# A three-stage float32 kernel on one core: one quad instead of two by whole float32 matmuls, and elementwise work of the first blocks on GpSimd

## The chip, the cores and the metric

The kernel runs on one core of a Trainium2 chip. The metric is the device time of one execution in microseconds, as the median of several runs. The profile is taken from one further execution; its span runs from the first to the last instruction of the core, and that execution's device time is a little longer than its span.

## The reference, cut to what matters

A linear attention is followed by two feed-forward networks. All inputs and the output are float32. B = 4 batches, H = 8 heads, S = 576 rows, D = 64; so 2304 tokens of 512 values go through two networks with 2048 hidden values.

```
q_s = softmax(q, over the head's 64 values);  k_s = softmax(k, over the sequence)
kv  = k_s^T v                  # 64 x 64 for each batch and head
x   = q_s kv                   # heads side by side: 2304 x 512
h1  = x @ w_in1 ; g1 = softplus(h1) ; y = g1 @ w_out1
h2  = y @ w_in2 ; g2 = elu(h2)      ; out = g2 @ w_out2
```

## The kernel before

The 2304 tokens are cut into six blocks of 384 rows, and two blocks make a pair (three pairs). The hidden values of a network are cut into eight quarters of 256, called f = 0 to 7. A **quad** (m, p, f) is the work of network m, pair p and quarter f: an up product (512 to 256 values, over the pair's two blocks), an activation, and a down product that adds into PSUM. There are 2 x 3 x 8 = 48 quads, and they follow each other in the order m, p, f; the down product of one quad is laid between the up products of the next.

An ordinary quad works with seven products in place of eight (a Strassen-like scheme). It needs seven *forms* of x for the pair (`add_forms`: four differences `ts`, line 599, and for each form a high part, line 588, and a low part, line 592, as the products are made from a rounded high part and a low remainder), seven forms of the up weights (`add_w_in`: four sums `st`, line 711, high parts by ScalarE, line 727, low parts by VectorE, line 731), a high and a low part of the down weights (`add_w_out`, lines 751 and 755), and of the activation (`add_g`, lines 940 and 944). Its up products (line 811) leave seven results that ScalarE copies (line 824) and VectorE adds (line 845).

A **direct** quad leaves all that out: `add_up_direct` (line 872) and the `whole` branch of `add_down` (line 1011) multiply float32 tiles as they are, and its activation stands in `g` alone. Before, the quads (0, 0, 0) and (0, 0, 1) are direct:

```
direct = lambda m, p, f: (m, p) == (0, 0) and f < 2
```

For the eight quarters of each network the weights are first turned from the words of the input into float32 by `add_words` (ScalarE lines 647 and 661, VectorE lines 651, 655 and 672); they come through the ring `raw` of two buffers. In network 0 the up forms are made anew for each pair from the turned words, and the down parts are stored in DRAM and loaded again.

Before the first quad the attention of block 0 must be done (`add_k`, `add_q` for four pairs of heads, each by itself), then that of block 1 (two units of four heads). In `add_q` the row maximum (line 439) is subtracted (line 446), ScalarE takes the exponential (line 452), VectorE sums (456) and multiplies by the reciprocal (line 476, `qn`). Block 0's subtractions are on GpSimd already, the rest of this is on VectorE. The values then pass through TensorE (lines 491 and 507) into `sx`, the pair's x.

All instructions are put in order by a planner (`Plan.order`), which simulates the engines with a duration for each step (`t_act`, `t_dve`, `t_pool`, `t_dma`) and takes the step that can start first, and among those that can start together the most urgent. `PRI` is a table of numbers that make groups of steps more urgent (k00 is k of block 0's heads 0 and 1, k12 the second unit of block 1, x00 the forms of pair 0, i0 to i7 and o0 to o7 the weights of a quarter). All DMAs are issued by SyncE, in the planned order. GpSimd has, beside the subtractions, the `memset` of line 304, which waits until TensorE has read the buffer `v` (line 375).

Of the kernel before, what the change touches and what calls it, by code (L numbers as in the profile page):

```python
# [12 lines left out]
ALU = mybir.AluOpType  # L13
# [132 lines left out]


def t_pool(n):
    return 0.15 + n / 476


def t_dma(n):
# [4 lines left out]
def attention_moe_moe_kernel(  # L157
# [93 lines left out]

    SLOT = 15.7
    UP, DN = 6 * 0.175, 3 * 0.231
    direct = lambda m, p, f: (m, p) == (0, 0) and f < 2
    quads = [(m, p, f) for m in range(2) for p in range(NPAIR) for f in range(NQ)]
    start, now = {}, 45.0
    for m, p, f in quads:
# [4 lines left out]
    def after_quad(m, p, f):  # L262
        i = quads.index((m, p, f)) + 1
        return start[quads[i]] if i < len(quads) else end


    kload = {}
# [147 lines left out]
    def add_q(t, hps, behind=()):  # L415
# [23 lines left out]
            nc.vector.tensor_reduce(new(qm)[:, : 2 * R * G], flat(), axis=AX.X, op=ALU.max)  # L439

        N = 2 * R * G
        eng = POOL if early else DVE

        @step(eng, 1.1 if early else t_dve(n), r=[qm], w=[qk])
        def _(eng=eng):
            (nc.gpsimd if eng == POOL else nc.vector).tensor_tensor(
                flat(), flat(), T[qm][:, :N].to_broadcast([P, N, D]), op=ALU.subtract
            )

# [18 lines left out]
        by = lambda t: t[:, :n].rearrange("p (g h r d) -> p g h r d", g=G, h=2, r=R)  # L468
        rows = lambda: T[qk][:, BLK:] if early else T[nk][:, :n]

        @step(DVE, t_dve(n), r=[qk, qd], w=[nk] if early else [], make=[] if early else [(nk, "u")])
        def _():
            if not early:
                new(nk)
            for g in range(G):
                nc.vector.tensor_tensor(
                    rows()[:, g * BLK : (g + 1) * BLK].rearrange("p (r h d) -> p h r d", h=2, r=R),
                    by(T[qk])[:, g],
                    T[qd][:, 2 * R * g : 2 * R * (g + 1)].rearrange("p (h r) o -> p h r o", h=2).to_broadcast([P, 2, R, D]),
                    op=ALU.mult,  # L480
                )
# [85 lines left out]
    def add_forms(m, p):  # L567

        t = (2 * p, 2 * p + 1)

        def b(i, j):
            return [("xs", m, t[j - 1], kc) for kc in (2 * i - 2, 2 * i - 1)], ("sx", m, t[j - 1]), (
                lambda: T["sx", m, t[j - 1]][:, (i - 1) * 2 * BLK : i * 2 * BLK]
            )

        def ts(i):
            key = ("ts", m, p, i)
            return [key], key, (lambda: T[key])

        def form(i, src):  # L580
            r, hold, view = src
            xk, hk, lk = (("x" + c, m, p, i) for c in "fhl")
            part = lambda j: T[xk][:, j * 2 * BLK : (j + 1) * 2 * BLK]

            @step(ACT, t_act(2 * BLK), r=r, w=[hk], make=[(xk, "xf")], hold=[hold], line="xf")
            def _():
                new(xk)
                nc.scalar.copy(part(0), view())

            @step(DVE, t_dve(2 * BLK), r=[*r, hk], w=[lk], hold=[xk, hold])  # L590
            def _():
                nc.vector.tensor_tensor(part(1), view(), part(0).bitcast(F32), op=ALU.subtract)

        def diff(i, one, two):
            key = ("ts", m, p, i)

            @step(DVE, t_dve(2 * BLK), r=[*one[0], *two[0]], make=[(key, "ts")], hold=[one[1], two[1]], line="ts")
            def _():
                nc.vector.tensor_tensor(new(key), one[2](), two[2](), op=ALU.subtract)

            return ts(i)

        form(1, b(1, 1))
        form(2, b(2, 1))
        t1 = diff(1, b(1, 2), b(1, 1))
        t2 = diff(2, b(2, 2), t1)
        form(6, t2)
        form(5, t1)
        form(3, b(2, 2))
        t3 = diff(3, b(2, 2), b(1, 2))  # L610
        form(7, t3)
        t4 = diff(4, b(2, 1), t2)
        form(4, t4)
# [78 lines left out]
    def add_w_in(m, p, f, rk):  # L692
# [9 lines left out]
            (3, lambda: a(1, 1), lambda: a(2, 1), ALU.subtract), (4, lambda: a(1, 2), lambda: s(2), ALU.subtract),  # L702
        ]
        for i, x, y, op in sums:
            @step(
                DVE, t_dve(W2), r=[rk], w=[] if i == 1 else [sk], make=[(sk, "st")] if i == 1 else [],
            )
            def _(i=i, x=x, y=y, op=op):
                if i == 1:
                    new(sk)  # L710
                nc.vector.tensor_tensor(s(i), x(), y(), op=op)

        view = lambda j, lo, n, c: T[wk][:, j * 7 * W2 + lo : j * 7 * W2 + lo + n].rearrange(
            "p (c n) -> p c n", c=c
# [138 lines left out]
    def add_up_direct(f):  # L853
        t0 = start[0, 0, f]
        wk = ("w", "ti", 0, "i", f)
        for t in range(2):
            gk = ("g", 0, 0, f, t)
            for j in range(2):
                key = ("up", f, t, j)
                for lo in range(0, KC, PART):  # L860
                    kcs = range(lo, lo + PART)

                    @step(
                        PE, PART * 0.645, r=[wk, *(("xs", 0, t, kc) for kc in kcs)], w=[key] if lo else [],
                        make=[] if lo else [(key, "ha")], hold=[("sx", 0, t)],
                        due=t0 + (4 * t + 2 * j + lo / 2) * (UP + 1.5 * DN), line=("up", t) if lo + PART == KC else None,
                    )
                    def _(key=key, j=j, t=t, kcs=kcs):
                        ps = T[key] if kcs[0] else new(key)
                        for kc in kcs:  # L870
                            lo = kc * W2 + j * P
                            nc.tensor.matmul(  # L872
                                ps[:, :BLK], T[wk][:, lo : lo + P], sx(0, t, kc),
                                start=(kc == 0), stop=(kc == KC - 1),
                            )

                last_up[0, 0, f] = _

                @step(
                    ACT, t_act(BLK, True), r=[key], w=[gk] if j else [],  # L880
                    make=[] if j else [(gk, "gh" if f else "g")], line=("g", t), tab="sp",
                )
                def _(key=key, gk=gk, j=j):
                    if not j:
                        new(gk, F32)
                    softplus(T[gk][:, j * BLK : (j + 1) * BLK], T[key][:, :BLK])
# [96 lines left out]

    def add_down(m, p, f):

        wk = ("wo", m, "o", f) if p == direct(m, 0, f) else ("wo", m, "o", f, p)
        t0 = after_quad(m, p, f)
        if turned(m, p):
            return add_down_turned(m, p, f, wk, t0)
# [4 lines left out]
        for (i, j, r), at in zip(order, fill):  # L994
# [2 lines left out]
            hk, lk, ak = ("gh", m, p, f, i), ("gl", m, p, f, i), ("acc", m, p, half, r)  # L997
            first = f == 0 and j == 0

            whole = direct(m, p, f)  # L1000
            gk, w32 = ("g", m, p, f, i), ("w", "ti", m, "o", f)

            @step(
# [18 lines left out]
    def add_store(m, p):  # L1022
# [55 lines left out]


    PRI = dict(  # L1080
        k00=97, q00=38, k01=54, q01=13, k02=167, q02=154, k03=94, q03=54, k10=9, q10=83, k12=24, q12=11,
        k20=157, q20=11, k22=95, q22=30, k30=136, q30=45, k32=30, q32=0, x00=6, x01=36, x02=32, x10=48, x11=48,
        x12=213, y=59, w=-34, ahead=148, i0=-2, i1=43, i2=48, i3=173, i4=-23, i5=52, i6=66, i7=17, o0=105,
        o1=26, o2=29, o3=-28, o4=45, o5=18, o6=-2, o7=10,
    )

    def early(kind):
# [25 lines left out]
    for i, (m, p, f) in enumerate(quads):  # L1113
# [8 lines left out]
            load_w_in(m, p, f)  # L1122
        if (m, p) == (0, 0):
            early(f"o{f}")
        if direct(m, p, f):
            add_words(m, "o", f, "wo")
        elif (m, p) == (0, 0):
            add_w_out(m, f, add_words(m, "o", f))
        elif p == (1 if direct(m, 0, f) else 0):
            add_w_out(m, f, load_words(m, p, "o", f))  # L1130
        else:
            load_w_out(m, p, f)
# [4 lines left out]
        early(None)  # L1137
        if direct(m, p, f):
            add_up_direct(f)
        else:  # L1140
            add_up(m, p, f)
            for j in range(2):
# [47 lines left out]
```

## Time and profile before

| | |
|---|---|
| median of 3 runs | 842.51 us (842.42 to 843.38) |
| the profiled execution | 843.36 us, its span 841.3 us |
| TensorE busy | 821.2 us (98% of the span) |
| VectorE, ScalarE, GpSimd busy | 590.1, 534.2, 6.1 us |

Busy shares are means over the whole span. The two networks don't load the engines alike, and the first pair, whose attention, forms and words fall together, loads VectorE and ScalarE far more than the rest; so the first 200 us are to be read by stages.

### The profile page before, as it was taken

How to read it: one execution, taken by the hardware profiler on the slowest of the kernel's cores; microseconds unless marked ns; L12 is line 12 of the kernel's file. 1: busy time of each engine (PE TensorE's matmuls, PEld its weight loads, DVE VectorE, ACT ScalarE, POOL GpSimd, SP SyncE). 2: the span in 40 equal slices, each digit the busy share in tenths (PEclk: the TensorE clock that was granted, in tenths of full speed). 3: DMA queues.
4: the chain of work that ended last, by engine and by line, in shares of the span. 5: the costliest groups of instructions: out<-in, count | busy, mean ns of one | idle time of the engine just before them, and what ended most of it. 6: DMA issues, size and time to landing. Idle time of an engine off the chain costs nothing.

```text
span 841.3 us, 11929 instructions
## 1 busy us (share of the span) xinstructions
PE 821.2 (98%) x4678; PEld 721.3 (86%) x4678; DVE 590.1 (70%) x910; ACT 534.2 (63%) x786; POOL 6.1 (1%) x28
## 2 busy tenths in 40 slices
PE   5799999999999999999999999999999999999998
PEld 4466788889989999999999999899888899888896
DVE  7889999988888768776776786776544556533433
ACT  3877988886887757656655665665534456534443
POOL 2000000000000000000000000000000000000000
PEclk9999999999999999999999999999999999999999
DMA  9687775537885654687756689673765453763532
GB/s 283 165 280 248 216 261 194 199 100 238 263 310 181 236 205 161 221 303 267 250 178 230 261 300 338 257 295 143 250 234 216 179 232 139 255 232 138 187 139 76
DMA packets 63575, 186.37 MB, mean 222 GB/s; under 512 B 17952, under 2 KB 27168, under 8 KB 54560
## 3 DMA queue, kind: packets, MB, share of 16 engines
q1 hardware_dynamic: 63520, 185.61, 63.2%
q8 instruction: 37, 0.61, 0.3%
q14 instruction: 18, 0.15, 0.1%
HBM read 131.07 MB, written 54.53 MB: 221 GB/s over the span
## 4 chain that ended last, share of the span: by engine, by line
PE 83%; DVE 9%; ACT 5%; DMA 2%; issue 2%; ACTq 0%; DVEq 0%; SPq 0%
PE acc L1016 27%; PE ub L811 21%; PE acc L978 15%; PE uc L811 11%; PE ua L811 5%; PE px L507 1%; DMA raw_i<-in_moe_w_in_dram 1%; DMA raw_o<-in_moe_w_out_dram 1%; DVE mt L331 1%; PE pk L375 1%; DVE wf_i L731 1%; PE up L872 1%; ACT kvbd L401 1%; DVE ti_o L655 1%; PE pq L491 1%
## 5 line engine op out<-in xcount | busy, mean ns | idle before, releaser
L811 PE MATMUL ub<-xf,wf_i 128*128 128x384 f32 x1104 | 226.7, 340 | 0.4 <-ACT s L824 0.3
L1016 PE MATMUL acc<-wo_o,gh 128*128 128x512 f32 x720 | 226.0, 395 | 0.0
L811 PEld LDWEIGHTS ub<-xf,wf_i 128*128 128x128 f32 x1104 | 193.4, 188 | 16.5 <-ACT s L824 2.8
L845 DVE TENSOR_TENSOR h<-uc,s 128x384 f32<-128x384 f32 x92 | 51.1, 555 | 143.4 <-PE uc L811 135.0
L1016 PEld LDWEIGHTS acc<-wo_o,gh 128*128 128x128 f32 x720 | 132.5, 188 | 18.8
L1016 PE MATMUL acc<-wo_o,gl 128*128 128x512 f32 x360 | 142.5, 396 | 0.0
L824 ACT COPY s<-ub 128x384 f32<-128x384 f32 x138 | 65.9, 478 | 106.8 <-PE ub L811 106.5
L811 PE MATMUL uc<-xf,wf_i 128*128 128x384 f32 x552 | 112.2, 338 | 0.6 <-ACT g L893 0.6
L978 PE MATMUL acc<-gh,wo_o 128*128 128x512 f32 (+1 forms) x512 | 111.4, 339 | 0.0
L811 PEld LDWEIGHTS uc<-xf,wf_i 128*128 128x128 f32 x552 | 96.6, 188 | 8.2 <-ACT g L893 1.4
L940 ACT CAST gh<-g 128x768 fp32r<-128x768 f32 x92 | 77.1, 839 | 37.8 <-DVE g L933 37.1
L944 DVE TENSOR_TENSOR gl<-g,gh 128x768 fp32r<-128x768 f32 x92 | 87.8, 954 | 18.2 <-ACT gh L940 17.8
L978 PEld LDWEIGHTS acc<-gh,wo_o 128*128 128x128 f32 x512 | 83.2, 188 | 7.1
L1016 PEld LDWEIGHTS acc<-wo_o,gl 128*128 128x128 f32 x360 | 67.5, 187 | 14.4
L978 PE MATMUL acc<-gl,wo_o 128*128 128x512 f32 (+1 forms) x256 | 65.4, 336 | 0.0
L811 PE MATMUL ua<-xf,wf_i 128*128 128x384 f32 x276 | 55.8, 336 | 0.0
L811 PEld LDWEIGHTS ua<-xf,wf_i 128*128 128x128 f32 x276 | 48.0, 188 | 1.4 <-ACT xq L497 0.3
L933 DVE SCALAR_TENSOR_TENSOR g<-h,u 128x768 f32<-128x768 f32 x48 | 45.9, 957 | 1.4
L978 PEld LDWEIGHTS acc<-gl,wo_o 128*128 128x128 f32 x256 | 39.1, 188 | 5.3
L921 ACT ACTIVATE u<-h 128x768 f32<-128x768 f32 x48 | 40.7, 848 | 4.5 <-DVE h L845 2.7
L731 DVE TENSOR_TENSOR wf_i<-st_i,wf_i 128x1024 fp32r<-128x1024 f32 x30 | 36.6, 1221 | 8.1 <-ACT wf_i L727 7.9
L925 ACT ACTIVATE u<-u 128x768 f32<-128x768 f32 x48 | 40.7, 847 | 1.1
(98 smaller groups left out, 937.1 us busy)
## 6 DMA issues: line engine op xcount, KB each, us to landing
wo_o<-wod SPq DMA_DIRECT2D x30, 1024.0 KB, 6.8
wf_i<-wfd SPq DMA_DIRECT2D x16, 1792.0 KB, 7.3
raw_i<-in_moe_w_in_dram SPq DMA_DIRECT2D x16, 1024.0 KB, 6.5
raw_o<-in_moe_w_out_dram SPq DMA_DIRECT2D x16, 1024.0 KB, 7.4
wod<-wo_o SPq DMA_DIRECT2D x16, 1024.0 KB, 6.2
wfd<-wf_i SPq DMA_DIRECT2D x8, 1792.0 KB, 9.0
r_i<-w32i SPq DMA_DIRECT2D x24, 512.0 KB, 5.5
w32i<-ti_i SPq DMA_DIRECT2D x14, 512.0 KB, 5.5
```

What stands on the lines that cost most here:

```text
L331: top = lambda o, x, y: nc.vector.tensor_tensor(o, x, y, op=ALU.max)
L731: nc.vector.tensor_tensor(view(1, lo, n, c), get(), view(0, lo, n, c).bitcast(F32), op=ALU.subtract)
L811: nc.tensor.matmul(ps[:, :BLK], T[wk][:, lo : lo + P], T[xk][:, (2 * c + kc) * BLK : (2 * c + kc + 1) * BLK], start=(i in first and kc == ...
L824: nc.scalar.copy(new(sk), T[key][:, :BLK])
L845: nc.vector.tensor_tensor(T[hk][:, half * BLK : (half + 1) * BLK], T[key][:, :BLK], T[sk], op=ALU.add)
L921: nc.scalar.activation(new(uk), T[hk], AF.Relu, scale=-1.0)
L925: nc.scalar.activation(T[uk], T[uk], AF.Exp, scale=-1.0)
L933: nc.vector.scalar_tensor_tensor(new(gk), T[hk], 0.0, T[uk], op0=ALU.max, op1=ALU.add)
L940: nc.scalar.copy(new(hk), T[gk])
L944: nc.vector.tensor_tensor(new(lk), T[gk], T[hk].bitcast(F32), op=ALU.subtract)
L978: nc.tensor.matmul(ps, T[wk][:, lo : lo + P], T[g][:, cols], start=(first and n == 0 and starts), stop=(f == NQ - 1 and j == 1 and n == 2) ...
L1016: nc.tensor.matmul(ps, T[g][:, col : col + P], T[wk][:, (2 * a + j) * DM : (2 * a + j + 1) * DM], start=(first and n == 0), stop=(f == NQ ...
```

## The change

One quad, not two, is direct: (0, 0, 1) becomes an ordinary quad, with forms of its up weights, with high and low parts of its down weights and activation, and with its down weights' parts stored for the pairs behind it. A table says which elementwise steps GpSimd takes: the subtractions of blocks 0 and 1 (`qs`), the normalising multiply of block 0 (`qn`), and the four differences of x for pair (0, 0) (`ts`). The sums of the up weights (`st`) could be put there too and are not. The planner's price of a GpSimd step is lower by 0.12 us, and the table `PRI` has other numbers, so that the whole order is planned anew.

```diff
 def t_pool(n):
-    return 0.15 + n / 476
+    return 0.03 + n / 476
...
-    direct = lambda m, p, f: (m, p) == (0, 0) and f < 2
+    direct = lambda m, p, f: (m, p) == (0, 0) and f < 1
+    whole_down = lambda m, p, f: (m, p) == (0, 0) and f < 1
...
+    ON_POOL = {"qs": (0, 1), "qn": (0,), "ts": ((0, 0),), "st": ()}
+
+    def elementwise(kind, where, n):
+        if where in ON_POOL[kind]:
+            return POOL, t_pool(n), nc.gpsimd
+        return DVE, t_dve(n), nc.vector
...
-        eng = POOL if early else DVE
-
-        @step(eng, 1.1 if early else t_dve(n), r=[qm], w=[qk])
+        eng, dur, nce = elementwise("qs", t, n)
+
+        @step(eng, dur, r=[qm], w=[qk])
...
-        @step(DVE, t_dve(n), r=[qk, qd], w=[nk] if early else [], make=[] if early else [(nk, "u")])
+        eng, dur, nce = elementwise("qn", t, n)
+
+        @step(eng, dur, r=[qk, qd], w=[nk] if early else [], make=[] if early else [(nk, "u")])
...
-                nc.vector.tensor_tensor(
+                nce.tensor_tensor(
                     rows()[:, g * BLK : (g + 1) * BLK].rearrange("p (r h d) -> p h r d", h=2, r=R),
...
-            @step(DVE, t_dve(2 * BLK), r=[*one[0], *two[0]], make=[(key, "ts")], hold=[one[1], two[1]], line="ts")
+            eng, dur, nce = elementwise("ts", (m, p), 2 * BLK)
+
+            @step(eng, dur, r=[*one[0], *two[0]], make=[(key, "ts")], hold=[one[1], two[1]], line="ts")
             def _():
-                nc.vector.tensor_tensor(new(key), one[2](), two[2](), op=ALU.subtract)
+                nce.tensor_tensor(new(key), one[2](), two[2](), op=ALU.subtract)
...
-                    make=[] if j else [(gk, "gh" if f else "g")], line=("g", t), tab="sp",
+                    make=[] if j else [(gk, "gh" if f and whole_down(0, 0, f) else "g")], line=("g", t), tab="sp",
...
-            whole = direct(m, p, f)
+            whole = whole_down(m, p, f)
...
     PRI = dict(
-        k00=97, q00=38, k01=54, q01=13, k02=167, q02=154, k03=94, q03=54, k10=9, q10=83, k12=24, q12=11,
-        k20=157, q20=11, k22=95, q22=30, k30=136, q30=45, k32=30, q32=0, x00=6, x01=36, x02=32, x10=48, x11=48,
-        x12=213, y=59, w=-34, ahead=148, i0=-2, i1=43, i2=48, i3=173, i4=-23, i5=52, i6=66, i7=17, o0=105,
-        o1=26, o2=29, o3=-28, o4=45, o5=18, o6=-2, o7=10,
+        k00=31, q00=51, k01=143, q01=75, k02=9, q02=189, k03=18, q03=24, k10=18, q10=194, k12=19, q12=171,
+        k20=108, q20=64, k22=104, q22=32, k30=123, q30=23, k32=75, q32=11, x00=52, x01=27, x02=32, x10=194,
+        x11=11, x12=-14, y=157, w=-46, ahead=36, i0=-100, i1=53, i2=11, i3=-27, i4=-22, i5=175, i6=91, i7=-18,
+        o0=90, o1=38, o2=35, o3=-4, o4=-7, o5=30, o6=34, o7=217,
     )
...
-        if direct(m, p, f):
+        if whole_down(m, p, f):
             add_words(m, "o", f, "wo")
         elif (m, p) == (0, 0):
             add_w_out(m, f, add_words(m, "o", f))
-        elif p == (1 if direct(m, 0, f) else 0):
+        elif p == (1 if whole_down(m, 0, f) else 0):
             add_w_out(m, f, load_words(m, p, "o", f))
```

## Rows read from the trace of the kernel before

**Rows 1.** The page: its first line and the engines' busy time.
```profile
span 841.3 us, 11929 instructions
PE 821.2 (98%) x4678; PEld 721.3 (86%) x4678; DVE 590.1 (70%) x910; ACT 534.2 (63%) x786; POOL 6.1 (1%) x28
```

**Rows 2.** Busy time by stretch: length, then each engine's, clock, DMA.
```profile
3.70:33.40 29.70, 20.38 (x276) 15.43 (x277) 27.98 (x79) 17.39 (x32) 3.45 (x5) 1.00 0.75 232
...
33.40:128.50 95.10, 92.31 (x495) 64.94 (x495) 88.99 (x132) 79.78 (x108) 0.29 (x2) 1.00 0.81 253
33.40:184.40 151.00, 147.86 (x831) 112.53 (x831) 138.62 (x210) 126.26 (x179) 0.43 (x3) 1.00 0.70 221
```

**Rows 3.** The chain that ended last, late in the run: start, length, what.
```profile
656.47 1.06 PE ub L811 x6
...
672.16 1.06 PE ub L811 x6
```

**Rows 4.** The same chain between 60 and 131 us, two of its pieces.
```profile
72.62 8.15 DMA raw_o<-in_moe_w_out_dram
...
115.07 9.40 DMA raw_i<-in_moe_w_in_dram
```

**Rows 5.** Timeline of TensorE and its weight loads, 40 to 65 us.
```profile
46.32 2.32 PE L375 MATMUL pk<-v,k 64*64 64x65 f32 x72
...
54.74 1.46 PE L507 MATMUL px<-xq,kvbd 128*128 128x192 f32 x8
...
56.90 7.90 PE L872 MATMUL up<-sx,w_ti_i 128*128 128x384 f32 x24
64.64 1.88 PE L1011 MATMUL acc<-w_ti_o,g 128*128 128x512 f32 x4
...
43.22 0.19 PEld L1011 LDWEIGHTS acc<-w_ti_o,g 128*128 128x128 f32 x1 [0.24 <-issue]
43.65 0.19 PEld L1011 LDWEIGHTS acc<-w_ti_o,g 128*128 128x128 f32 x1 [0.24 <-issue]
```

**Rows 6.** Groups of instructions by line and shape, GpSimd and VectorE.
```profile
L446 POOL TENSOR_TENSOR q<-q,qm 128x384 f32<-128x384 f32 x4 | 3.3, 830 | 17.8 <-DVE qm L439 16.9 <-DVE qd L461 0.9
...
L944 DVE TENSOR_TENSOR gl<-g,gh 128x768 fp32r<-128x768 f32 x92 | 87.8, 954 | 18.2 <-ACT gh L940 17.8
...
L731 DVE TENSOR_TENSOR wf_i<-st_i,wf_i 128x1024 fp32r<-128x1024 f32 x30 | 36.6, 1221 | 8.1 <-ACT wf_i L727 7.9
...
L651 DVE TENSOR_SCALAR ti_i<-raw_i 128x1024 uint32<-128x1024 uint32 x16 | 11.0, 688 | 5.0 <-ACT raw_i L647 4.9
...
L711 DVE TENSOR_TENSOR st_i<-ti_i 128x256 f32<-128x256 f32 x12 | 5.0, 420 | 0.0
L731 DVE TENSOR_TENSOR wf_i<-ti_i,wf_i 128x512 fp32r<-128x512 f32 x6 | 4.1, 689 | 0.1
...
L476 DVE TENSOR_TENSOR q<-q,qd 128x384 f32<-128x384 f32 x4 | 2.2, 556 | 0.0
```

**Rows 7.** The same for ScalarE.
```profile
L940 ACT CAST gh<-g 128x768 fp32r<-128x768 f32 x92 | 77.1, 839 | 37.8 <-DVE g L933 37.1
L824 ACT COPY s<-ub 128x384 f32<-128x384 f32 x138 | 65.9, 478 | 106.8 <-PE ub L811 106.5
...
L727 ACT CAST wf_i<-st_i 128x1024 fp32r<-128x1024 f32 x30 | 31.5, 1051 | 4.8 <-DVE st_i L711 4.8
```

**Rows 8.** Timeline of GpSimd and VectorE near 17 us.
```profile
16.80 0.83 POOL L446 TENSOR_TENSOR q<-q,qm 128x384 f32<-128x384 f32 x1 [0.93 <-DVE qd L461]
...
17.52 0.56 DVE L476 TENSOR_TENSOR q<-q,qd 128x384 f32<-128x384 f32 x1
```

**Rows 9.** Timeline of VectorE and TensorE where up weights become ready.
```profile
70.00 1.22 DVE L731 TENSOR_TENSOR wf_i<-st_i,wf_i 128x1024 fp32r<-128x1024 f32 x1
...
110.42 1.22 DVE L731 TENSOR_TENSOR wf_i<-st_i,wf_i 128x1024 fp32r<-128x1024 f32 x1
...
112.11 1.22 PE L811 MATMUL ub<-xf,wf_i 128*128 128x384 f32 x6
```

More of the change, by code (lines that the diff above doesn't have):

```diff
@@ L441, in add_q, with _ @@
         N = 2 * R * G
-        eng = POOL if early else DVE
-        @step(eng, 1.1 if early else t_dve(n), r=[qm], w=[qk])
-        def _(eng=eng):
-            (nc.gpsimd if eng == POOL else nc.vector).tensor_tensor(
+        eng, dur, nce = elementwise("qs", t, n)
+        @step(eng, dur, r=[qm], w=[qk])
+        def _(nce=nce):
+            nce.tensor_tensor(
                 flat(), flat(), T[qm][:, :N].to_broadcast([P, N, D]), op=ALU.subtract
@@ L469, in add_q, with _ @@
         rows = lambda: T[qk][:, BLK:] if early else T[nk][:, :n]
-        @step(DVE, t_dve(n), r=[qk, qd], w=[nk] if early else [], make=[] if early else [(nk, "u")])
-        def _():
+        eng, dur, nce = elementwise("qn", t, n)
+        @step(eng, dur, r=[qk, qd], w=[nk] if early else [], make=[] if early else [(nk, "u")])
+        def _(nce=nce):
             if not early:
@@ L475, in _ @@
             for g in range(G):
-                nc.vector.tensor_tensor(
+                nce.tensor_tensor(
                     rows()[:, g * BLK : (g + 1) * BLK].rearrange("p (r h d) -> p h r d", h=2, r=R),
@@ L704, in add_w_in, with _ @@
         for i, x, y, op in sums:
+            eng, dur, nce = elementwise("st", (m, p), W2)
             @step(
-                DVE, t_dve(W2), r=[rk], w=[] if i == 1 else [sk], make=[(sk, "st")] if i == 1 else [],
+                eng, dur, r=[rk], w=[] if i == 1 else [sk], make=[(sk, "st")] if i == 1 else [],
             )
-            def _(i=i, x=x, y=y, op=op):
+            def _(i=i, x=x, y=y, op=op, nce=nce):
                 if i == 1:
                     new(sk)
-                nc.vector.tensor_tensor(s(i), x(), y(), op=op)
+                nce.tensor_tensor(s(i), x(), y(), op=op)
         view = lambda j, lo, n, c: T[wk][:, j * 7 * W2 + lo : j * 7 * W2 + lo + n].rearrange(
@@ L984, in add_down @@
     def add_down(m, p, f):
-        wk = ("wo", m, "o", f) if p == direct(m, 0, f) else ("wo", m, "o", f, p)
+        wk = ("wo", m, "o", f) if p == whole_down(m, 0, f) else ("wo", m, "o", f, p)
         t0 = after_quad(m, p, f)
@@ L1139, in attention_moe_moe_kernel @@
             add_up_direct(f)
+            for t in range(0 if whole_down(m, p, f) else 2):
+                add_g(m, p, f, t)
         else:
```

## The prediction, made before the changed kernel was run

> **What bounds the kernel now.** I read the page first: TensorE is busy for 98% of the span [rows 1], so time can come out of this kernel only where TensorE waits or where its own work gets less. Next the chain of what ended last. Late in the run it holds nothing but matmuls, and the quads follow each other at one period: 672.16 - 656.47 = 15.69 us [rows 3]. There nothing changes for the edit. Early it is another picture: between 60 and 131 us the chain runs over VectorE steps and over two loads of raw weights, 8.15 and 9.40 us [rows 4], though TensorE is hardly ever idle. The table by stretch says how near the two engines stand to each other. From 3.7 to 33.4 us, ahead of the first up product, VectorE is busy for 27.98 of 29.70 us and TensorE for 20.38: VectorE sets the start. From 33.4 to 128.5 us TensorE is busy for 92.31 of 95.10 us and VectorE for 88.99, so VectorE has 6.1 us to spare. From 33.4 to 184.4 us, where pair 1 begins, VectorE has 151.00 - 138.62 = 12.4 us to spare, and TensorE 3.1 [rows 2]. So the first 184 us have two bounds that are almost level, and the change takes from the one and gives to the other. Behind 184 us TensorE is alone, and whatever has been won or lost by then stays to the end.
>
> **TensorE's work: -4.95 us.** A direct quad has 16 up matmuls of 384 columns and 12 down matmuls of 512; each shows as two records. 24 up records run from 56.90 to 64.64 us, 0.3225 us each; 32 of them are 10.3 us. Down records follow each other every 0.43 us (43.22 to 43.65); 24 of them are 10.3 us [rows 5]. A direct quad is thus 20.64 us, an ordinary one 15.69 us [rows 3]. One quad changes its kind: -4.95 us. This is work on the engine with the highest share, so it counts wholly where VectorE keeps pace.
>
> **The start: -2.0 us.** In the stretch up to 33.4 us VectorE loses block 0's four multiplies, 4 x 0.556, and one subtraction of block 1 of 768 elements, for which I take the 0.954 us of another VectorE operation of that shape [rows 6]: 3.2 us. GpSimd takes them. For 384 elements its row is 0.830 us; 768 elements are not in the trace. They lie between 0.83 and twice that, 1.66; VectorE's own price grows by 0.954/0.556 = 1.72 from the one size to the other, which would make 1.42; I take 1.6, near the upper end. Each of the multiplies stands in its head pair's chain and becomes 0.27 us longer there, but only the last one's delay can reach the first up product. Bounds: nothing gained (the loads, or the words of the first up weights, end last) and all 3.2 us. I take 2.0, since VectorE has just 1.7 us of idle time in that stretch [rows 2].
>
> **What VectorE and ScalarE get.** Quad (0, 0, 1) now needs four sums (4 x 0.42), low parts of three pieces of the up weights (0.69, 0.42 for 256 elements as in the sums, 1.22), a low part of the down weights (1024 elements, 1.22), three additions of 384 elements (3 x 0.556, as the multiplies) and two low parts of the activation (2 x 0.954) [rows 6]: 1.68 + 2.33 + 1.22 + 1.67 + 1.91 = 8.8 us for VectorE. Behind 33.4 us GpSimd takes from it the second subtraction of block 1 and the four differences, 5 x 0.954 = 4.8 us. Net +4.0 us. ScalarE gets casts of the up weights (at most 2 x 1.05, as the two smaller pieces are together no longer than the large one), one of the down weights (1.05), three copies (3 x 0.478) and two high parts (2 x 0.839) [rows 7], 6.3 us in all. It has 151.00 - 126.26 = 24.7 us to spare up to 184.4 us [rows 2]; I cost that at nothing, and without this cover it could cost 6.3.
>
> **Can VectorE keep pace: +2.5 us.** It must find 4.0 us more in a time that is 4.95 us shorter, 8.95 us. Up to 184.4 us it has 12.4 to spare, so in the long run it can, with 3.4 left: lower bound 0. Up to 128.5 us it has 6.1, so 2.9 are missing, unless preparation of pair 1 is put back. Two places can be checked. First, where direct work ends. TensorE has then 20.64 of direct matmuls, at least 2.32 and 1.46 us for block 1's attention [rows 5], and two of quad 1's seven products that need block 0 only (1.06 us each [rows 3]): 26.5 us, so from 31.4 us it runs dry at 57.9. Before, the first ordinary quad's weights were ready at 71.2 us [rows 9]. In front of them stood words that can now come later (the second down weights, the third up weights, part of the third down weights: three shifts of 0.69 and five operations of 1024 elements, 1.22 each [rows 6], 8.2 us), and four operations that go to GpSimd (3.8 us): 71.2 - 12.0 = 59.2 us. This is 1.3 us late, with up to 1.3 us more because two differences in a row take 1.6 us each on GpSimd where they took 0.95. Second, quad (0, 0, 4): its last weights were ready at 111.64 us and used at 112.11 [rows 9]. TensorE would now ask for them some 5 to 7 us earlier, and VectorE must have put other things behind them. Time lost at the first place is time that VectorE gains for the second, so the two are not added: between 0 and 2.9 for the lack, 1.3 to 2.6 for the first place; I take 2.5.
>
> **Costed at nothing.** The stored down parts of quarter 1 replace a store and a load of its words and move 512 KB more on one side and as much less on the other; a DMA fewer is issued on SyncE. The loads of raw weights on the chain [rows 4] are gated by the words' buffers: a VectorE that is later makes them later too, and this is in the 2.5. GpSimd's queue holds its steps behind the memset that waits for TensorE to read `v`; it has some 13 us of new work (4 x 0.83 + 6 x 1.6) in about 45 us, and nothing but these steps is behind it.
>
> **Do GpSimd and VectorE hold each other up?** The GpSimd subtraction from 16.80 to 17.63 us overlaps a VectorE multiply of two SBUF tensors that starts at 17.52 by 0.11 us, and the multiply takes its usual 0.56 [rows 8]. That is all the trace has; the other VectorE work beside GpSimd's reads one SBUF tensor and PSUM, or reduces. In the stretches where the new GpSimd work falls, most VectorE work reads two. The bounds are 0 and the whole of GpSimd's new time, 12.9 us, of which 8.0 is behind 33.4 us. I take 0, the nearest row. The Trainium skill (SBUF — State Buffer, "Who interferes with whom") says that such a VectorE instruction contends with a GpSimd instruction that reads SBUF, and that the later of the two blocks until the other is through; by that rule the sum goes from about -4.5 towards the slower rival below, and the 0.11 us of overlap is too short to tell.
>
> **The sum.** -4.95 - 2.0 + 2.5 = -4.45 us. The profiled execution took 843.36 us (span 841.3, 2.06 around it), which becomes 838.9; it stands 0.85 above the median of the runs, so the median becomes 838.1 us. I say 838.2. The measurement tells about 0.2% (1.7 us) from no change.
>
> **The rivals.** *VectorE gives nothing away* (everything fits): -4.95 - 3.2 + 0 = -8.15 us, 834.4. For it: 12.4 us of slack. Against it: the 1.3 us at the end of the direct work and the missing 2.9. *VectorE is the clock up to 128 us:* the chain runs over it and not over TensorE there. TensorE's 4.95 us then turn into waits, the start gives 2.0, and VectorE's 4.0 us more take half of its slack and come out at about 2: 842.5, no change. Against it: TensorE idles for only 2.8 us in that stretch now. *Slower, by one mechanism:* GpSimd's reads and VectorE's two-tensor operations take turns. VectorE then stands still for up to 8.0 us behind 33.4 us and the gain of the start is gone. The lack is 8.0 - 3.4 = 4.6 us if all can be put back, 2.9 + 8.0 = 10.9 if nothing can, 7.8 in the middle: -4.95 + 7.8 = +2.85 us, 845.4. From a lack of 6.7 us on the change is slower by over 0.2%. The Trainium skill's rule above is what speaks for it; the 0.56 us at 17.52 speaks faintly against it [rows 8].
>
> **Chances and range.** The forecast (836 to 840.7) 0.50, everything fits 0.13, no change 0.17, slower 0.20. Faster by over 0.2% takes the first two and a little of the third, 0.66; within 0.2% 0.14; slower 0.20. A range from 835.0 to 845.3 leaves out half of the second case and somewhat over half of the fourth, under 0.2.
>
> **What will show it.** The first up product (line 872) starts near 31.4 us; later than 33 and the start's term is wrong. The first down product of an ordinary quad and pair 1's first up product come 4 to 5 us earlier than before (pair 1: near 180 us). TensorE's idle time between 58 us and 128 us grows by 2 to 3 us, with waits for VectorE's forms or weights; beyond 7 us the slower rival holds. VectorE operations beside GpSimd's differences keep their 0.95 to 1.22 us; if they or GpSimd's grow, or gaps open in front of them, the two take turns. Behind 184 us the period stays at 15.69 us. The prediction is wrong if TensorE's work isn't 5 us less, or if the new order leaves more idle time late in the run.

## The result, and the profile after

The changed kernel takes 850.62 us (849.71 to 850.89), the kernel before 842.89 us beside it: ratio 1.009 (95% interval 1.0072 to 1.0107). It is 7.7 us slower, where 838.2 us was predicted: the sign is wrong, and the time lies outside the range.

The page of the changed kernel, its first line, the engines' busy time and the row of granted clocks (40 slices):

```profile
span 849.1 us, 12014 instructions
PE 823.2 (97%) x4700; PEld 728.0 (86%) x4700; DVE 598.9 (71%) x912; ACT 531.7 (63%) x789; POOL 21.2 (2%) x38
...
PEclk9699999999999999999999999999999999999999
```

Against [rows 1] the span is 7.8 us longer. TensorE's busy time should have fallen by 4.95 us and rose by 2.0; its idle time (span less busy) rose from 20.1 to 25.9 us. The second slice of the clock is low. The table by stretch, for the stretches of [rows 2] and then three shorter ones:

```profile
3.70:33.40 29.70, 19.45 (x262) 14.38 (x262) 26.29 (x73) 16.82 (x30) 8.20 (x11) 0.89 0.80 240
33.40:128.50 95.10, 88.67 (x560) 67.03 (x561) 91.83 (x131) 75.87 (x112) 10.77 (x8) 0.94 0.73 231
33.40:184.40 151.00, 144.40 (x836) 115.98 (x837) 143.29 (x209) 123.36 (x178) 10.77 (x8) 0.97 0.67 219
...
24.00:28.00 4.00, 2.02 (x10) 0.90 (x10) 3.11 (x9) 3.10 (x8) 0.90 (x2) 0.86 0.72 238
28.00:34.00 6.00, 3.37 (x40) 2.71 (x40) 5.79 (x13) 4.07 (x5) 0.00 (x0) 0.50 0.58 188
34.00:41.00 7.00, 6.04 (x18) 4.15 (x18) 6.72 (x9) 4.33 (x8) 1.80 (x1) 0.54 1.10 266
```

From 33.4 to 128.5 us TensorE idles for 6.4 us where it idled for 2.8, while VectorE is busy for 91.8 of 95.1. On top of that TensorE's granted clock was 0.50, its lower level (1.2 GHz), from 28 to 34 us, behind 4 us in which it had been busy for only half the time; before, it was 1.00 throughout. Late in the run nothing has changed: from 300 us to the end TensorE idles for 4.1 us, before for 3.9. The chain of what ended last there (start, length, what):

```profile
649.31 1.04 PE ua L826 x6
...
665.00 1.04 PE ua L826 x6
```

The period is 15.69 us, as in [rows 3]. Where the time goes is seen where GpSimd's new work lies. The timelines of VectorE and of GpSimd in the changed kernel (start, length, instruction, idle time before it and what ended it):

```profile
23.05 1.62 DVE L603 TENSOR_TENSOR xf<-sx,xf 128x768 fp32r<-128x768 f32 x1 [0.74 <-ACT xf L599]
...
38.63 2.38 DVE L668 SCALAR_TENSOR_TENSOR ti_o<-raw_o,ti_o 128x1024 uint32<-128x1024 uint32 x1
...
51.98 2.04 DVE L726 TENSOR_TENSOR st_i<-ti_i,st_i 128x256 f32<-128x256 f32 x1
53.95 2.31 DVE L664 TENSOR_SCALAR ti_o<-raw_o 128x1024 uint32<-128x1024 uint32 x1
...
61.44 2.57 DVE L603 TENSOR_TENSOR xf<-sx,xf 128x768 fp32r<-128x768 f32 x1
...
67.72 2.23 DVE L340 TENSOR_TENSOR mt<-mt 128x256 f32<-128x256 f32 x2
69.99 0.29 DVE L340 TENSOR_TENSOR mx<-mt,k 128x128 f32<-128x128 f32 x1
```

```profile
51.84 1.90 POOL L612 TENSOR_TENSOR ts<-sx,sx 128x768 f32<-128x768 f32 x1 [11.91 <-ACT sx L531]
53.82 1.88 POOL L612 TENSOR_TENSOR ts<-sx,ts 128x768 f32<-128x768 f32 x1
60.53 2.67 POOL L612 TENSOR_TENSOR ts<-sx 128x768 f32<-128x768 f32 x1 [4.83 <-DVE xf L603]
...
67.17 2.18 POOL L612 TENSOR_TENSOR ts<-sx,ts 128x768 f32<-128x768 f32 x1 [3.90 <-DVE xf L603]
```

Each of the four differences has beside it one VectorE instruction (the last a pair in one row) that starts behind it and ends 0.3 to 0.8 us after it: a sum of 256 elements takes 2.04 us and not 0.42, a shift 2.31 and not 0.69 [rows 6], a low part 2.57 and not 0.95. Two more are like that ahead of 40 us (a low part of 1.62 at 23.05, a two-input instruction on the words of 2.38 at 38.63, which takes 1.22 elsewhere). The six are stretched by 1.62 + 1.62 + 1.62 + 1.48 + 0.67 + 1.16 = 8.2 us, 7.5 of them behind 33.4 us. What this does to TensorE is plain at 70 us. Its timeline there:

```profile
66.66 1.02 PE L1026 MATMUL acc<-w_ti_o,g 128*128 128x512 f32 x2
70.33 0.33 PE L348 MATMUL pt<-ident,mx 128*128 128x128 f32 x1 [2.65 <-DVE mx L340]
70.42 1.60 PE L826 MATMUL ub<-xf,wf_i 128*128 128x384 f32 x6
71.95 0.70 PE L360 MATMUL pb<-ident,m 128*64 128x128 f32 x4
```

The pair of maxima at 67.72 takes 2.23 us beside GpSimd's difference; in the kernel before it takes 0.75:

```profile
69.00 0.75 DVE L331 TENSOR_TENSOR mt<-mt 128x256 f32<-128x256 f32 x2
```

The last maximum `mx` is late by that, and TensorE stands for 2.65 us in front of the transpose that reads it. Its clock falls again (0.66 from 70 to 75 us): the four matmuls of line 360 take 0.70 us, and the same four took 0.44 before.

### The profile page after: what moved, and what is told of

Same layout as the page of the kernel before. It is cut to its first block, busy times and chain, and to the rows that moved or that the text cites. A ratio compares the mean times of both kernels' runs of the same rounds, so it can differ in the third digit from the quotient of the medians.

```text
span 849.1 us, 12014 instructions
## 1 busy us (share of the span) xinstructions
PE 823.2 (97%) x4700; PEld 728.0 (86%) x4700; DVE 598.9 (71%) x912; ACT 531.7 (63%) x789; POOL 21.2 (2%) x38
## 4 chain that ended last, share of the span: by engine, by line
PE 86%; DVE 8%; ACT 4%; issue 1%; DMA 0%; POOL 0%; DVEq 0%; POOLq 0%; ACTq 0%
PE acc L1031 29%; PE ub L826 22%; PE acc L993 14%; PE uc L826 11%; PE ua L826 5%; PE px L518 1%; DVE mt L340 1%; DVE xf L603 1%; PE pk L384 1%; PE pq L502 1%; PE acc L1026 1%; DVE wf_i L746 1%; ACT L908 0%; DVE wo_o L770 0%; DVE st_i L726 0%
## 5 line engine op out<-in xcount | busy, mean ns | idle before, releaser
L1031 PE MATMUL acc<-wo_o,gh 128*128 128x512 f32 x744 | 233.9, 395 | 0.0
L826 PE MATMUL ub<-xf,wf_i 128*128 128x384 f32 x1128 | 230.5, 339 | 2.6 <-ACT s L839 2.3
L826 PEld LDWEIGHTS ub<-xf,wf_i 128*128 128x128 f32 x1128 | 197.3, 188 | 18.9 <-ACT s L839 5.0
L1031 PEld LDWEIGHTS acc<-wo_o,gh 128*128 128x128 f32 x744 | 136.7, 188 | 19.3 <-issue 0.2
L1031 PE MATMUL acc<-wo_o,gl 128*128 128x512 f32 x372 | 147.2, 396 | 0.0
L839 ACT COPY s<-ub 128x384 f32<-128x384 f32 x141 | 67.7, 480 | 116.1 <-PE ub L826 115.6
L826 PE MATMUL uc<-xf,wf_i 128*128 128x384 f32 x564 | 115.6, 339 | 0.8 <-DVE h L860 0.7
L826 PEld LDWEIGHTS uc<-xf,wf_i 128*128 128x128 f32 x564 | 98.9, 188 | 9.0 <-DVE h L860 2.1
L959 DVE TENSOR_TENSOR gl<-g,gh 128x768 fp32r<-128x768 f32 x94 | 89.7, 954 | 12.3 <-ACT gh L955 11.9
L1031 PEld LDWEIGHTS acc<-wo_o,gl 128*128 128x128 f32 x372 | 69.7, 187 | 15.3 <-DVE gl L959 0.4
```

Of the source, the lines that this page charges most:

```text
L826: nc.tensor.matmul(ps[:, :BLK], T[wk][:, lo : lo + P], T[xk][:, (2 * c + kc) * BLK : (2 * c + kc + 1) * BLK], start=(i in first and kc == ...
L839: nc.scalar.copy(new(sk), T[key][:, :BLK])
L959: nc.vector.tensor_tensor(new(lk), T[gk], T[hk].bitcast(F32), op=ALU.subtract)
L1031: nc.tensor.matmul(ps, T[g][:, col : col + P], T[wk][:, (2 * a + j) * DM : (2 * a + j + 1) * DM], start=(first and n == 0), stop=(f == NQ ...
```

## The experiments

All ratios are to the kernel before, run on the same chip. A difference between two runs is the difference of their ratios times 843 us, or that of their medians where they ran on one chip and this is said. "First up" is the start of the first up product, "last ua" that of the last quad's `ua` product; both are read from TensorE's timeline. "First up" tells of the start only where the same work stands ahead of it: in e7 and e10 all of block 1's `pk` products do (288 records on TensorE, 216 in the kernel before, the changed one, e3 and e12).

| kernel | median us | ratio (95%) | first up | last ua |
|---|---|---|---|---|
| before | 842.89 | 1 | 33.40 | 814.55 |
| changed | 850.62 | 1.009 (1.0072 to 1.0107) | 39.04 | 821.98 |
| e3 changed, ten steps as fills | 842.87 | 0.9994 (0.9985 to 1.0004) | 37.53 | 814.36 |
| e6 the same, `ts` fills wait | 843.84 | 1.0006 (0.9997 to 1.0016) | 37.28 | 814.38 |
| e4 changed, ten steps on VectorE | 847.43 | 1.0047 (1.0032 to 1.0063) | 39.32 | 818.13 |
| e5 before, ten steps on GpSimd | 847.92 | 1.0055 (1.004 to 1.007) | 34.55 | 819.83 |
| e11 before, ten steps as fills | 843.34 | 1.000 (0.9991 to 1.0009) | 32.68 | 814.76 |
| e7 one direct quad, nothing moved | 843.68 | 1.000 (0.9991 to 1.001) | 44.24 | 815.54 |
| e10 e7, ten steps as fills | 845.51 | 1.0026 (1.0017 to 1.0035) | 44.95 | 817.67 |
| e9 changed, other order | 847.63 | 1.0044 (1.0029 to 1.006) | 36.41 | 818.57 |
| e8 e9, ten steps as fills | 841.40 | 0.9973 (0.996 to 0.9985) | 36.05 | 812.10 |
| e12 e3, fillers on TensorE | 841.72 | 0.9985 (0.9976 to 0.9994) | 36.43 | 813.67 |
| e13 changed, fillers on TensorE | 850.33 | 1.0083 (1.0066 to 1.01) | 38.84 | 822.94 |

The "ten steps" are those that the change gives to GpSimd: block 1's two subtractions, block 0's four multiplies, the four differences. Where they are "fills" their results are replaced by constants: two fills each take about GpSimd's time and read nothing.

**e3: GpSimd busy as long, but reading nothing.** The edit to the differences; block 1's `qs` and block 0's `qn` are edited in the same way.

```diff
-                nce.tensor_tensor(new(key), one[2](), two[2](), op=ALU.subtract)
+                if nce is nc.gpsimd:
+                    dst = new(key)
+                    for _i in range(2):
+                        nce.memset(dst, 0.5)
+                    return
...
```

> The changed kernel in its own order; the ten operations that are new on GpSimd (block 1's two subtractions, block 0's four multiplies, pair 0's four differences) are replaced by fills of the same outputs, two each, so that GpSimd writes and reads nothing there (that part of the attention and of the forms is left out). Turn-taking theory (GpSimd instructions that read SBUF and VectorE instructions with two SBUF inputs hold each other off): no VectorE operation is stretched any more (subtractions 0.95 us, words 0.69 and 1.22 us), the 8 us of stretch go, and the time falls from 850.6 to 840 to 843.5 us. Order theory (the new order puts block 1 ahead and starts the direct quad late, whatever GpSimd does): the first up product stays at 38 to 39 us and the time at 847 us or more. Late-forms theory (VectorE's 4 us more): 847 us or more too, with TensorE waiting near 68 us.

0.9994: the whole loss is gone, 8.1 us. No VectorE instruction is stretched by more than 0.3 us any more (one on six columns takes 0.46 us and not 0.17 beside fills). The table by stretch, as above:

```profile
3.70:33.40 29.70, 18.13 (x263) 13.85 (x263) 27.52 (x77) 16.08 (x29) 7.98 (x16) 0.92 0.90 250
33.40:128.50 95.10, 92.98 (x596) 73.20 (x597) 90.57 (x137) 82.88 (x120) 7.97 (x13) 0.97 0.76 246
33.40:184.40 151.00, 148.72 (x873) 121.82 (x874) 141.53 (x217) 130.22 (x189) 7.97 (x13) 0.98 0.67 221
```

From 33.4 to 128.5 us TensorE idles for 2.1 us, no more than before. The fills of the differences waited for nothing here and came too early (the first at 38.6 us), so part of the gain could be dependencies gone; e6 asks for that.

**e6: the fills wait as the differences did.** Ahead of its fills each difference subtracts two columns of its own sources.

```diff
+                    nce.tensor_tensor(dst[:, ::BLK], one[2]()[:, ::BLK], two[2]()[:, ::BLK], op=ALU.subtract)
```

> As the run with fills, but each difference of pair 0 first subtracts two columns of its two sources on GpSimd, so that the fills wait for the same sources as the differences did (in the run with fills they waited for nothing and could come early; the differences, the subtractions of block 1 and the multiplies of block 0 are left out but for these columns). Turn-taking theory: within 1.5 us of the run with fills, 842 to 844.5. If the early fills were what made that run fast: 846 us or more.

1.0006: 7.1 us better than the changed kernel, 1.0 worse than e3. So about 1 us of e3's gain was missing waits, and the reads cost 7.1. In this price is also that two fills are shorter than a difference, by some 0.3 us each time (1.58 and 1.87 us in the small kernel below).

**e4: the changed kernel's order, with the ten steps issued on VectorE.**

```diff
-            return POOL, t_pool(n), nc.gpsimd
+            return POOL, t_pool(n), nc.gpsimd if (kind, where) == ("qs", 0) else nc.vector
```

> The changed kernel in its own order, with the same ten operations issued on VectorE at their places in that order. Turn-taking theory: no stretch, but VectorE has 7.9 us more of its own (4 x 0.556 + 6 x 0.954), which is what turn-taking cost it; so about the changed kernel's time, 848 to 852 us. If GpSimd had really taken work off VectorE, this kernel would be slower than the changed one by 5 us or more, 855 us and above.

1.0047, 847.43 us, a little below the 848 to 852 that were expected. VectorE making all ten itself is 3.6 us faster than GpSimd making them: the help is worse than none. Against e6 the same run says that VectorE's load counts in this order: rid of the ten steps without GpSimd's reads, the kernel is 3.5 us faster (1.0047 to 1.0006).

**The price by itself.** A small kernel, a stage at a time: six GpSimd subtractions of 768 elements, alone and beside VectorE instructions of several kinds.

```python
gt = lambda: nc.gpsimd.tensor_tensor(po, a, b, op=ALU.subtract)   # 128 x 768, all SBUF
tt = lambda: nc.vector.tensor_tensor(vo, a, b, op=ALU.subtract)   # two SBUF inputs
tp = lambda: nc.vector.tensor_tensor(vo[:, :384], ps, a[:, :384], op=ALU.add)  # one in PSUM
tr = lambda: nc.vector.tensor_reduce(mx, a.rearrange("p (n d) -> p n d", d=64), axis=AX.X, op=ALU.max)
ts = lambda: nc.vector.tensor_scalar(wo, w, 3, None, op0=ALU.logical_shift_left)
```

> No part of the reference is computed: seven stages, each started only when the one before is through. GpSimd subtractions of 128x768 alone; VectorE subtractions of 128x768 from two SBUF tensors alone; both together; GpSimd beside VectorE additions of PSUM and SBUF; beside VectorE reductions; GpSimd fills beside VectorE subtractions; GpSimd beside VectorE shifts of 1024 words. Turn-taking theory: 1.64 and 0.95 us alone; together each waits for the other, so that six and eight of them take the sum of both (near 17 us) where they would take 10; beside PSUM additions, reductions and with fills nobody is longer than alone; beside the shifts the two take turns again. No-contention theory: every stage takes the longer of its two engines' own times.

Its timeline, a row for each engine and stage (start, total length, instruction, how many):

```profile
3.36 11.19 POOL L56 TENSOR_TENSOR po<-a,b 128x768 f32<-128x768 f32 x6 [2.06 <-DVE po L48]
...
14.78 7.91 DVE L52 TENSOR_TENSOR vo<-a,b 128x768 f32<-128x768 f32 x8
...
22.98 16.79 DVE L52 TENSOR_TENSOR vo<-a,b 128x768 f32<-128x768 f32 x8
23.10 14.87 POOL L56 TENSOR_TENSOR po<-a,b 128x768 f32<-128x768 f32 x6 [8.54 <-DVE a L39]
...
40.11 11.21 POOL L56 TENSOR_TENSOR po<-a,b 128x768 f32<-128x768 f32 x6 [2.14 <-DVE a L39]
40.13 7.07 DVE L53 TENSOR_TENSOR vo<-psa,a 128x384 f32<-128x384 f32 x12
...
51.55 7.87 DVE L54 TENSOR_REDUCE mx<-a 128x12 f32<-128x768 f32 x8
51.59 11.21 POOL L56 TENSOR_TENSOR po<-a,b 128x768 f32<-128x768 f32 x6 [0.27 <-DVE a L39]
...
63.04 7.91 DVE L52 TENSOR_TENSOR vo<-a,b 128x768 f32<-128x768 f32 x8
63.06 9.48 POOL L57 MEMSET po<- 128x768 f32 x12 [0.25 <-DVE a L39]
...
72.66 17.57 DVE L55 TENSOR_SCALAR wo<-w 128x1024 uint32<-128x1024 uint32 x12
72.82 13.21 POOL L56 TENSOR_TENSOR po<-a,b 128x768 f32<-128x768 f32 x6 [0.28 <-DVE a L39]
```

Alone (beside one reduction) the six take GpSimd 11.19 us and eight two-input subtractions take VectorE 7.91. Side by side they take 14.87 and 16.79. Beside additions from PSUM, beside reductions and (fills) when GpSimd only writes, nobody is slowed. The shift reads one tensor and is slowed all the same: 12 take 17.57 us, where 12 of 0.688 [rows 6] are 8.3. So each GpSimd subtraction of 768 elements holds VectorE for (16.79 - 7.91) / 6 = 1.48 us, and spares it the 0.954 us of making the result itself: a loss of about 0.5 us on VectorE, whenever VectorE has such work at the time.

**e5 and e11: GpSimd's part alone.** The kernel before, its two direct quads and its order; only the engine that issues the ten steps is changed. In e11 they are waiting fills on GpSimd. The edit of e5 to the differences, with `qs` and `qn` edited likewise:

```diff
-                nc.vector.tensor_tensor(new(key), one[2](), two[2](), op=ALU.subtract)
+                (nc.vector if m or p else nc.gpsimd).tensor_tensor(new(key), one[2](), two[2](), op=ALU.subtract)
...
```

> The kernel before, with both direct quads and its own order; only the ten operations (block 1's two subtractions, block 0's four multiplies, pair 0's four differences) are issued on GpSimd in place of VectorE. Turn-taking theory: in the stage runs above a GpSimd operation of 768 elements took about 1.5 us of VectorE's time where it spares 0.95, so moving loses up to 0.5 us each, six times, and the multiplies of 384 elements lose little; where the operation's result is waited for, 0.7 us more each. The time goes up by 2 to 6 us, 845 to 849. If GpSimd's help is real where VectorE sets the pace, the time falls by 1 us or more below 842.9.

> The kernel before in its own order, with two direct quads, relieved of the same ten operations in the same way (the same parts left out). VectorE-limit theory: TensorE has 4.95 us more here, so the relief is worth less, 0 to 2 us: 841 to 843.5, above the relieved one-quad run by 1.5 to 4 us. If VectorE alone set the pace in both: as much below the kernel before as the relieved one-quad run is below the one-quad run.

1.0055 and 1.000: the offload alone costs 4.6 us, all of it by its reads. In e5 the same pairs are seen, of VectorE and then of GpSimd:

```profile
60.73 2.71 DVE L655 SCALAR_TENSOR_TENSOR ti_i<-raw_i,ti_i 128x1024 uint32<-128x1024 uint32 x1
...
66.57 2.32 DVE L731 TENSOR_TENSOR wf_i<-ti_i,wf_i 128x512 fp32r<-128x512 f32 x1
```

```profile
60.22 2.13 POOL L599 TENSOR_TENSOR ts<-sx,ts 128x768 f32<-128x768 f32 x1
66.46 1.89 POOL L599 TENSOR_TENSOR ts<-sx 128x768 f32<-128x768 f32 x1 [4.10 <-DVE xf L592]
```

e11 says a second thing. There VectorE was rid of the ten steps, and the kernel became no faster. With two direct quads and this order VectorE's load alone did not set the time; but two fills take longer than VectorE's own step (1.58 us for 0.95), and what waits for them waits longer, so a bound by VectorE isn't ruled out.

**e7 and e10: the one direct quad alone.** Only block 0's subtractions stay on GpSimd, and `PRI` is chosen anew for that. In e10 the ten steps are waiting fills in the order of e7.

```diff
-    ON_POOL = {"qs": (0, 1), "qn": (0,), "ts": ((0, 0),), "st": ()}
+    ON_POOL = {"qs": (0,), "qn": (), "ts": (), "st": ()}
```

> One direct quad, but only block 0's subtractions on GpSimd, as before; the table of urgencies is chosen anew for this kernel, so that the order fits it. VectorE-limit theory (TensorE's 4.95 us come back as waits because VectorE has 8.8 us more in a stretch where it is as full as TensorE): no gain, 841.5 to 845 us. If TensorE's work counts as the prediction's sum had it and only GpSimd spoiled it: 837 to 840 us.

> The run with one direct quad and its own order; the ten operations are taken off VectorE and replaced by fills on GpSimd that wait for the same sources (block 1's subtractions, block 0's multiplies and pair 0's differences are left out but for two columns of each difference). VectorE has 7.9 us less, TensorE the same. VectorE-limit theory: the time falls by 2.5 to 5 us, 838.5 to 841.5. If VectorE is not what holds the one-quad kernel: within 1 us of it, 842.7 to 844.7.

1.000: one direct quad in place of two, with an order chosen for it, gives nothing. I took VectorE for the reason; then e10 should have been faster, and it is 2.2 us slower, outside both of its ranges, though VectorE is busy for only 19.65 of the 26.6 us from 33.4 to 60 us (25.22 in e7). Less work on VectorE alone doesn't help in this order. The theory isn't disproved by it, as the fills take longer than the steps that they replace: from 56 to 70 us the chain of what ended last runs over `ts` fills for 2.6 us, and in e7 over no GpSimd step.

**e9 and e8: another order.** The changed kernel with another `PRI` (e9), and the same with waiting fills (e8).

```diff
-        k00=31, q00=51, k01=143, q01=75, k02=9, q02=189, k03=18, q03=24, k10=18, q10=194, k12=19, q12=171,
+        k00=63, q00=83, k01=40, q01=-20, k02=9, q02=108, k03=240, q03=63, k10=10, q10=133, k12=19, q12=111,
...
```

> The changed kernel with that same table of urgencies and all its work. Turn-taking theory: the order can't take it away; 5 to 9 us slower than the run with fills in this order, 845 to 850 us. If the changed kernel's order was the main loss: within 2 us of that run.

> The run with fills that wait (block 1's subtractions, block 0's multiplies and pair 0's differences left out but for two columns of each difference), with another table of urgencies, chosen for the case that GpSimd and VectorE don't touch each other. If the changed kernel's own order is what kept the run with fills at no gain: 838 to 841.5 us. If the engines' loads do it whatever the order: 842.5 to 845 us.

847.63 and 841.40 us, on one chip: the reads cost 6.2 us in this order too. The order has a price of its own: by the ratios e9 is 3.9 us faster than the changed kernel with the same work, and e8 2.8 us faster than e6. Without the reads this order is 0.27% faster than the kernel before, the best that was seen, and it leaves ten results out. Of the kernels that leave nothing out, none beats the one before.

**e12 and e13: does the clock cost, or is it a by-product?** Transposes of the identity into an unused corner of the PSUM tile stand ahead of the products at which TensorE waited; they need nothing but the tile. e12 is e3 with them, e13 the changed kernel. Six stand ahead of each `pt` (shown) and `pb` of block 1, ten ahead of the first `pq` of a unit of block 1 and of block 0's last.

```diff
+            for _i in range(6 if t == 1 else 0):
+                nc.tensor.transpose(p[:, 2 * P : 3 * P], ident, ident)
             nc.tensor.transpose(p[: n * D, :P], T[mx][:, : n * D], ident)
```

> The order of the changed kernel with the ten new GpSimd steps as fills (as in the third experiment's sense: no reads, no turn-taking), plus idle-time filler on TensorE: 6 transposes of the identity into an unused corner of the same PSUM tile ahead of block 1's pt and pb products, and 10 ahead of block 0's last pq and of each unit's first pq of block 1. They wait for nothing but the tile, so they run where TensorE stood waiting for VectorE or GpSimd between 24 and 34 us, and the real operands come no later. In the fills kernel the granted clock was 0.50 from about 28 to 39 us, and TensorE was busy at it for some 8 us. Theory A (the low clock follows the idle gaps and costs time that is kept to the end): the clock stays at 1.00 from 24 to 41 us, the matmuls there take half as long, the first up product starts 1 to 3 us earlier than 37.53, and the time is 839 to 841.5 us where the fills gave 842.87. Theory B (the clock costs nothing, as TensorE waits for VectorE there anyhow): the clock is higher, the gaps grow by as much, and the time stays within 0.15% of 842.9. Theory C (the fillers delay real products): 843.5 to 845 us.

> The changed kernel with all its work, and the same idle-time filler on TensorE (6 transposes ahead of block 1's pt and pb, 10 ahead of block 0's last pq and of each unit's first pq of block 1). In the changed kernel the clock was 0.50 from about 27 to 41 us, behind idle gaps of 1.68 and 1.89 us at 25 and 28 us. Theory A (the clock costs time that is kept): clock near 1.00 from 24 to 41 us, first up product 1 to 3 us earlier than 39.04, time 847 to 849 us where the changed kernel took 850.6. Theory B (VectorE and GpSimd in turns set the pace, the clock is a by-product): 850 to 851.5 us. Theory C (the fillers delay real products): 852 us or more.

e12, by stretch, as in the changed kernel's table:

```profile
24.00:28.00 4.00, 3.88 (x32) 3.06 (x30) 3.66 (x12) 3.45 (x9) 1.61 (x4) 1.00 0.64 176
28.00:34.00 6.00, 3.60 (x52) 2.82 (x52) 5.82 (x12) 5.02 (x6) 0.00 (x0) 1.00 1.01 287
34.00:41.00 7.00, 6.73 (x67) 4.92 (x69) 6.75 (x10) 5.02 (x8) 3.88 (x5) 1.00 0.93 256
```

The clock stays at 1.00 (2.4 GHz), and the first up product comes 1.1 us earlier than in e3. The time falls by 0.8 us by the ratios, whose intervals overlap (1.15 by the medians, of two chips). In e13 the clock is up to 1.00 from 24 to 34 us as well (0.50 from 28 on without the fillers), the first up product comes 0.2 us earlier, and the time stays: 850.33. But e13 kept the clock up for a part only: it was 0.76 from 34 to 41 us (0.54 without the fillers), and from 65 to 80 us, where no fillers stand, 0.77 (0.89). The six `px` products just ahead of the first up product take 2.93 us in e13 as in the changed kernel, and 1.56 in e12. So the clock was worth about 1 us where it was kept up throughout (e12), and up to 34 us, in the changed kernel, it is a by-product: a faster TensorE only waits longer there, and the `pt` product at 33.65 us in the changed kernel comes at 33.61 in e13. What the rest of its low clock costs was not tested.

## Why the prediction was wrong, by its own steps

**The step that failed** is "Do GpSimd and VectorE hold each other up? ... I take 0". They do: 7.1 to 8.1 us in the changed kernel (e6, e3), 6.2 in another order (e9 to e8), 4.6 with two direct quads (e5 to e11). This is the rival "slower, by one mechanism", to which 0.20 was given, and near its upper bound of 8.0 us of stretched VectorE time behind 33.4 us is what came (7.5). The 0.11 us of overlap in [rows 8] was no evidence: records of one engine, too, overlap by nearly as much (51.98 + 2.04 = 54.02, and the next VectorE instruction starts at 53.95). The cost was bounded only by nothing and everything, and between ends so far apart I took one end. Nor was it the only error: without the reads the kernel is as fast as the one before and no faster (e3, e6), still some 5 us above the forecast. The rule that I had from the Trainium skill (SBUF — State Buffer, "Who interferes with whom") holds here in each case tried: two SBUF inputs on VectorE are slowed (16.79 for 7.91), one input beside PSUM and reductions are not (7.07, 7.87), and GpSimd's fills don't slow a two-input subtraction (7.91). The same section says that a `tensor_scalar` can take the shared ports too; the shifts (17.57 us) agree.

The rival's own time, 845.4, was too low by 5.2 us. It kept the saving of 4.95 us whole and had no price for the later start, the clock and the late loss below; that is the second error.

**TensorE's work, -4.95 us.** As work it is right, but it does not reach the end. By the pages, e3's busy time is 818.6 us of a span of 841.1, before 821.2 of 841.3: 2.6 less busy, 2.4 more idle. What is missing to 4.95 is matmuls at half clock, from 28 to 39 us: in e12, with the clock kept up, TensorE is busy for 822.1 us, at least 6.7 of them with fillers alone, so its own work is 815.4 us or less. Even so the net gain in e12 is only 0.9 us of span.

**The start, -2.0 us.** Wrong in sign. The first up product starts at 39.04 us, not 31.4; without turn-taking at 37.53 (e3), with the clock up as well at 36.43 (e12), 3.0 us behind the old 33.40. "Later than 33 and the start's term is wrong", it said. VectorE was full there and stayed full (27.52 of 29.70 us in e3, [rows 2] 27.98): the time freed by GpSimd was filled with other steps by the new order, not given to block 0's chain. VectorE's subtraction on `k` of block 0's last head pair stands ahead of block 1's first one (22.89 us) in the kernel before, and 10 us behind it (16.37 us) in e3. That of block 0's last head pair, before and in e3:

```profile
13.47 0.74 DVE L358 TENSOR_TENSOR k<-k,pb 128x576 f32<-128x576 f32 x1
...
26.00 0.74 DVE L367 TENSOR_TENSOR k<-k,pb 128x576 f32<-128x576 f32 x1
```

I had read the start's length from VectorE's load and not from what the order does with it.

**What VectorE and ScalarE get.** Right in size: without turn-taking VectorE's busy time from 33.4 to 184.4 us is 142.53 us in e12, 3.9 above [rows 2]; 4.0 was forecast. That it comes so near is in part luck, as the stretch doesn't hold quite the same work in both: over the whole run it is 1.5 us more (591.6 and 590.1), where the forecast's terms make 0.8. ScalarE had 151.00 - 123.36 = 27.6 us to spare, and its 6.3 are hidden.

**Can VectorE keep pace, +2.5 us.** Yes, when it isn't held up: in e12 TensorE idles 2.14 us from its first up product, at 36.43, to 184.4 us ([rows 2], from 33.4: 3.14), and 1.25 us of fillers lie there, in the way or in what would be a gap: between -1.0 and +0.3 us in place of 2.5.

**A loss that no term had.** From 184.4 to 300 us the new order costs another 1.1 us: TensorE is busy for 114.47 of 115.60 us in the changed kernel and 114.44 in e3 and e12, 115.51 before; with one direct quad in e7's order it is 115.60. The longest of these waits, 0.7 us, is for the addition `h`. The text named "more idle time late in the run" as a way to be wrong, at no price.

So e12 adds up: -4.95 + 3.0 (start) + 1.1 (late) and between -1.0 and +0.3 (middle) is between -1.85 and -0.55 us, and its span is 0.9 shorter.

**GpSimd's prices.** 1.6 us was taken for 768 elements. It is 1.64 with a repeated operand (the mean of one of 1.47 and one of 1.80 us) and, alone in the small kernel, 1.87 with two whole ones; beside VectorE's two-input work the differences took up to 2.67. The view by shape, of the changed kernel, GpSimd alone (what, busy us, mean ns):

```profile
L612 POOL TENSOR_TENSOR ts<-sx,ts 128x768 f32<-128x768 f32 x2 | 4.1, 2032 | 4.0 <-DVE xf L603 3.9
...
L487 POOL TENSOR_TENSOR q<-q,qd 128x384 f32<-128x384 f32 x4 | 3.3, 830 | 5.4 <-DVE rs L397 2.6 <-DVE qd L475 1.9 <-DVE qd L470 0.9
...
L455 POOL TENSOR_TENSOR q<-q,qm 128x768 f32<-128x768 f32 x2 | 3.3, 1636 | 11.6 <-DVE qm L448 11.5
```

GpSimd's idle time ahead of these ends with VectorE's results: its queue was not a bound, as costed.

**What stays open.** Why one direct quad alone gives nothing (e7): e10 speaks against VectorE's load there, e4 against e6 speaks for it in the changed kernel's order, and the order that was chosen can't be told from the change. Whether an order exists in which the 4.95 us come through without GpSimd's reads was not tried beyond e7.

## What to carry to other kernels

Before a step is moved to GpSimd, list what VectorE runs at that moment: beside two-input work on SBUF, or the shift, the step of 768 elements holds VectorE for longer (1.48 us) than it spared it (0.95), while beside reductions or reads of PSUM it is free. A cost with bounds of 0 and 8 us and one overlap of 0.11 us as evidence is a reason for a wide range, not for the value 0. And a saving on the busiest engine has to be followed to the last quad: the order planned anew gave most of it back, at the start and once more between 184 and 300 us.

## What was not expected of the hardware

TensorE's granted clock fell to 0.50 just behind an idle gap of 1.68 us (changed kernel, 24.9 to 26.6 us), and again around 71 us behind one of 2.65 us; and yet keeping the first spell away gained about 1 us in e12 and nothing that shows in e13, where it was kept away in part. And a plain shift with one SBUF input is held up by GpSimd's reads just as a two-input subtraction is: 17.57 us for twelve.
